# Linear attention and a gated FFN on one core: output weights loaded earlier, one undivided output projection for block 0, and an attention output tile laid out in column halves

## The chip, the core and the metric

The kernel runs on one NeuronCore of a Trainium2 chip. The metric is device time in microseconds, from launch to the end of the core's program. A profiled execution gives a trace of one run: its span is the time from the first to the last instruction that the profiler recorded. In the trace, PE is TensorE (PEld its weight loads), DVE is VectorE, ACT is ScalarE, POOL is GpSimd and SP is SyncE, which here only issues DMA transfers.

## The reference

There are two parts. The first is linear attention with decay, for batch 4, 8 heads, 768 positions and head size 64. With lam a decay of each head:

```python
for b in range(nb):
    intra = einsum('bhic,bhjc->bhij', qb, kb) * Dmask       # Dmask[i, j] = lam ** (i - j) for i >= j, else 0
    intra = einsum('bhij,bhjd->bhid', intra, vb)
    inter = einsum('bhid,bhde->bhie', qb * lam ** (pos + 1), kv_state)
    out[:, :, block b] = intra + inter
    kv_state = lam ** block * kv_state + einsum('bhsd,bhse->bhde', kb * lam ** (block - 1 - pos), vb)
```

The second part takes the attention output as x, with 3072 tokens (4 x 768) of 512 features (8 heads x 64):

```python
gate = 1 / (1 + exp(-(x @ w_gate)))      # w_gate: 512 x 1536
val = x @ w_val                          # w_val:  512 x 1536
out = (gate * val) @ w_out               # w_out:  1536 x 512
```

All inputs and the output are float32; the kernel computes with bfloat16 operands and accumulates in float32.

## The kernel before

**Tiling.** The sequence is cut into six blocks of 128 positions (n = 0 to 5), and a block is done for all four batches b together, so that a block has 512 tokens: batch b fills columns 128b to 128b + 127. The reference's block of 64 is an arrangement of its own; 128 gives the same function. Heads go in pairs, and the two heads of a pair use rows 0 to 63 and 64 to 127 of TensorE.

**Attention of a block** has these pieces. `t_` transposes k or q of two batches on TensorE (tk, tq in PSUM), `e_k` and `e_q` copy them out, to KS by ScalarE and to QS, with the decay factors, by VectorE. From block 2 on a DMA transpose (`xbar`, kt and qt) takes the place of `t_`. `piece_s` makes the scores (sp), `piece_m` multiplies them with the decay mask (MT, VectorE). `piece_i` multiplies q with the state Sb, `piece_a` adds scores times v (both into op), `piece_x` copies op to XT, the FFN's input, and `piece_c` makes the state's increment (cp) from v and from k scaled by `piece_kd` (kd, ScalarE). The list `att(n)` runs `piece_i`, `piece_a`, `piece_x` and `piece_c` in this order.

**FFN of a block.** There are 12 tiles of 128 hidden features. `piece_gv` (L343) makes one of them: four matmuls of 128x128 weights with 512 tokens into gp, four more into vp, a sigmoid by ScalarE (sg), and the product sg times vp by VectorE (ht). `piece_po` (L376) is the output projection: for each of four token tiles tt it accumulates 12 matmuls of 512 columns, one for each ht, into po, copies the sum to ob, and stores it from SP's DMA queue.

**Memory.** PSUM has two pools: ps_at with five buffers for attention and ps_ff with three for gp, vp and po. A new tile of a pool takes the buffer of the tile that came five or three tiles earlier, and waits until this has been read. Weights stay in SBUF: WG (gate), WV (value), WO (output).

**What sets the order.** The kernel fixes it by hand. Each engine runs its instructions in the order in which the program issues them; there is no planner. From L485 on, the order is a list `plan` of units: a unit is one `piece_gv` or one `piece_po`, with a list of further pieces that are issued right behind it. So attention of block n + 1 is threaded between the FFN tiles of block n.

**Loads.** Nearly all go through GpSimd's DMA queue, which casts float32 to bfloat16. They are issued in the order of the program and land in that order. The order of interest is that of L453 to L468: gate and value weights of the last tiles, block 1's k and q of batches 0 and 1, output weights 0 to 5, block 1's other k, q and v, output weights 6 to 11, then block 2's k and q. In blocks 1 to 5, k and q of batches 2 and 3 are loaded with the heads of a pair exchanged, in two transfers (L98). `next_loads` (L476) transposes a block's k and q by DMA from SP, then lets GpSimd wait for these (`gate`) and load v and the next k and q.

**The head.** Block 0 has no state. L399 to L449 run its attention with filler matmuls (`zeros`) between pieces, and end with batch 3 in two halves (ops), whose copies go to ScalarE and VectorE. Then `swap_halves` makes lamqs, lamq with the two 64-row halves exchanged, which `e_q` of block 1 uses.

**Around block 1.** In the plan (L530 to L571) block 1's first transposes and scores stand behind tiles 10 and 11 of block 0. Block 0's projection is cut in two: the first six hidden tiles (`lo`) of each token tile are projected right after block 0's tiles, with block 1's remaining attention between them, and copied to ob. The last six (`hi`) are projected behind block 1's second tile, and VectorE adds them to ob (L385). Block 0's stores are issued later, behind block 1's tile 3. Block 1's first tile is made in two column halves (L348): gate and value of columns 0 to 255, then of 256 to 511, since VectorE's copies of batches 2 and 3 come later than ScalarE's of 0 and 1.

Of the kernel before, what the change touches and what calls it, by code (L numbers as in the profile page):

```python
# [16 lines left out]
def kernel(  # L17
# [11 lines left out]
    nc = tc.nc  # L29
# [72 lines left out]
    def load_g(f0, f1):  # L102
        nc.gpsimd.dma_start(out=WG[:, :, f0 * 128:f1 * 128], in_=wg_r[:, :, f0 * 128:f1 * 128])  # L103

    def load_v(f0, f1):
        nc.gpsimd.dma_start(out=WV[:, :, f0 * 128:f1 * 128], in_=wv_r[:, :, f0 * 128:f1 * 128])  # L106
# [5 lines left out]
    def load_wo(f0, f1):  # L112
        nc.gpsimd.dma_start(out=WO[:, f0:f1], in_=wo_r[:, f0:f1])  # L113
# [94 lines left out]
    def tables_late():  # L208
        nc.scalar.activation(pk, lnl, AF.Exp, scale=jn[:, 0:1])
        nc.scalar.activation(kds, lnl, AF.Exp, scale=jn[:, 1:2])  # L210
        nc.scalar.activation(dec2, lnp, AF.Exp, scale=float(C))

    def swap_halves():
        ps = ps_at.tile([128, HP, C], FP32, name="lqs", tag="ps")
        nc.tensor.matmul(ps, lhsT=swap, rhs=lamq, start=True, stop=True)
        nc.vector.tensor_copy(lamqs, ps)

    def make_mask(u):
        nc.vector.tensor_tensor(
# [91 lines left out]

    def piece_x(n, bs, eng=None):
        if n not in XT:
            XT[n] = xtp.tile([128, NMT, B, C], BF16, tag="XT", name="XT")
        for b in bs:
            e = eng or (nc.vector if n < FIRST_XBAR and b >= NB2 else nc.scalar)
            (e.tensor_copy if e is nc.vector else e.copy)(XT[n][:, :, b, :], OP[n, b])  # L317

    def piece_c(n, hps):
        p, t = (ps_at, "ps") if n else (ps_ff, "ff")  # L320
        cp = p.tile([128, len(hps), B, 64], FP32, name="cp", tag=t)
        for i, hp in enumerate(hps):
            for b in range(B):
                for w in range(2):
                    h = 2 * hp + w
                    nc.tensor.matmul(cp[rows_of(half(b, h)), i, b, :],  # L326
                                     lhsT=KD[n][:, b, slot(n, b, h), :], rhs=T_["v", n][:, b, h, :],
                                     start=(i == 0 and b == 0), stop=(i == len(hps) - 1 and b == B - 1),
                                     skip_group_check=True)
        if n == 0:  # L330
            nc.scalar.copy(Sb[:, hps[0]:hps[-1] + 1], cp)
            return
        for i, hp in enumerate(hps):
            for at, d in ((slice(0, NB2), dec), (slice(NB2, B), decs)):
                nc.vector.scalar_tensor_tensor(  # L335
                    out=Sb[:, hp, at, :], in0=Sb[:, hp, at, :], scalar=d[:, hp:hp + 1],
                    in1=cp[:, i, at, :], op0=ALU.mult, op1=ALU.add)
# [4 lines left out]

    def piece_gv(n, ft):  # L343
        fs = slice(ft * 128, (ft + 1) * 128)
        x = XT[n].rearrange("p m b c -> p m (b c)")
        gp = ps_ff.tile([128, TCH], FP32, name="gp", tag="ff")
        parts = [slice(0, TCH)]
        if (n, ft) == (1, 0):  # L348
            parts = [slice(0, TCH // 2), slice(TCH // 2, TCH)]

        def product(ps, W, part):
            for mt in range(NMT):
                nc.tensor.matmul(ps[:, part], lhsT=W[:, mt, fs], rhs=x[:, mt, part],  # L353
                                 start=(part is parts[0] and mt == 0),
                                 stop=(part is parts[-1] and mt == NMT - 1), skip_group_check=True)

        product(gp, WG, parts[0])
        if len(parts) == 2:
            vp = ps_ff.tile([128, TCH], FP32, name="vp", tag="ff")
            product(vp, WV, parts[0])  # L360
            product(gp, WG, parts[1])
        sg = htp.tile([128, TCH], BF16, tag="sg", name="sg", bufs=3)
        nc.scalar.activation(sg, gp, AF.Sigmoid)  # L363
        if len(parts) == 1:
            vp = ps_ff.tile([128, TCH], FP32, name="vp", tag="ff")
        product(vp, WV, parts[-1])
        HT[n, ft] = htp.tile([128, TCH], BF16, tag="ht", name="ht", bufs=2 * NFT)
        nc.vector.tensor_mul(HT[n, ft], sg, vp)  # L368

    OB = {}  # L370

    def store(n, tt, c0=0, c1=DM):
        nc.sync.dma_start(out=out[tt * S + n * C:tt * S + (n + 1) * C, c0:c1],
                          in_=OB[n, tt][:, c0:c1])

    def piece_po(n, tt, c0, c1, eng, fts):  # L376
        if (n, tt) not in OB:
            OB[n, tt] = osb.tile([128, DM], FP32, tag="ob", name="ob")
        po = ps_ff.tile([128, DM], FP32, name="po", tag="ff")
        for ft in fts:  # L380
            nc.tensor.matmul(po[:, :c1 - c0], lhsT=HT[n, ft][:, tt * 128:(tt + 1) * 128],  # L381
                             rhs=WO[:, ft, c0:c1], start=(ft == fts[0]), stop=(ft == fts[-1]))
        o = OB[n, tt][:, c0:c1]
        if fts[0]:
            nc.vector.tensor_tensor(out=o, in0=o, in1=po[:, :c1 - c0], op=ALU.add)  # L385
        else:
            (eng.copy if eng is nc.scalar else eng.tensor_copy)(o, po[:, :c1 - c0])  # L387
        if n:
            store(n, tt, c0, c1)

# [2 lines left out]
    def zeros(m):  # L395
        for _ in range(m):
            nc.tensor.matmul(zps, lhsT=Sb[:, 0, 0:2, :], rhs=Sb[:, 0:2], start=True, stop=True)  # L397
# [38 lines left out]
    for b in range(3):  # L436
        piece_a(0, [b])
        piece_x(0, [b], nc.vector if b == 2 else nc.scalar)
    zeros(1)
    ops = [ps_at.tile([128, HP // 2, C], FP32, name="op", tag="ps") for _ in range(2)]  # L440
    for g in range(2):
        for hp in range(2 * g, 2 * g + 2):
            for w in range(2):
                nc.tensor.matmul(ops[g][rows_of(w), hp % 2, :], lhsT=T_["v", 0][:, 3, 2 * hp + w, :],
                                 rhs=MT[0, 3][:, w, hp, :], start=(hp % 2 == 0), stop=(hp % 2 == 1),
                                 skip_group_check=True)
    nc.scalar.copy(XT[0][:, 0:2, 3, :], ops[0])
    nc.vector.tensor_copy(XT[0][:, 2:4, 3, :], ops[1])
    swap_halves()  # L449

    for n in range(2):  # L453
        make_kd(n)
    load_gv(6, 8)
    load_g(8, 12)
    load_v(8, 10)
    load_v(10, 12)
    load(1, "k", 0, 2)
    load(1, "q", 0, 2)  # L460
    load_wo(0, 3)
    load_wo(3, 6)
    load(1, "k", 2, 4)
    load(1, "q", 2, 4)
    load(1, "v", 0, 2)
    load(1, "v", 2, 4)
    load_wo(6, 12)
    load(2, "kq")  # L468

    gates = const.tile([128, 2], BF16, tag="gates")  # L470
# [28 lines left out]
    def m_(n, b):  # L499
        return lambda: piece_m(n, b)  # L500

    def trans(n, bp):
        def go():
            bs = [2 * bp, 2 * bp + 1]
            t_("k", n, bs)
            e_k(n, bs)
            t_("q", n, bs)
            e_q(n, bs)
        return go
# [22 lines left out]
        behind[ft] = [kd(0, 2 * ft)]  # L532
    behind[1].append(lambda: make_mask(0))
    behind[3].append(lambda: make_mask(1))
    behind[10] = [trans(1, 0), kd(1, 0, 2, parts=[0])]
    behind[11] = [pair(piece_s, 1, 0), m_(1, 0), m_(1, 1), kd(1, 2, 6, parts=[0])]
    for ft in range(NFT):
        gv(0, ft, *behind[ft])
    lo, hi = range(NFT // 2), range(NFT // 2, NFT)
    po(0, 0, kd(1, 6, 8, parts=[0]), kd(1, 0, 2, parts=[1]), fts=lo)  # L540
    po(0, 1, t_k(1, [2, 3]), kd(1, 2, 5, parts=[1]), fts=lo, eng=nc.vector)
    po(0, 2, t_q(1, [2, 3]), pair(piece_c, 0, 0), pair(piece_c, 0, 1), kd(1, 5, 8, parts=[1]),
       pair(piece_s, 1, 1), m_(1, 2), m_(1, 3), fts=lo)
    po(0, 3, att(1), fts=lo)

    for n in range(1, NSTEP):
        nx = n + 1
        more = [[] for i in range(NFT)]
        if nx < NSTEP:
            more[3] = [lambda nx=nx: e_q(nx, [0, 1])]  # L550
            more[4] = [pair(piece_s, nx, 0), m_(nx, 0)]
            more[5] = [m_(nx, 1), lambda nx=nx: e_q(nx, [2, 3])]
            more[7] = [pair(piece_s, nx, 1), m_(nx, 2)]
            more[8] = [m_(nx, 3)]
            more[11] = [att(nx)]
        if nx < NSTEP - 1:
            for i in range(4):
                more[6 + i].append(kd(nx, 2 * i))
            more[5].append(lambda nx=nx: make_kd(nx))
        if n == 1:  # L560
            more[4:11] = more[3:10]
            more[3] = []
            more[2].append(lambda: next_loads(2))
            more[3].extend([lambda tt=tt, j=j: store(0, tt, 256 * j, 256 * j + 256)
                            for tt in range(B) for j in range(2)])
            more[8].append(lambda: next_loads(3))
        for ft in range(NFT):
            gv(n, ft, *more[ft])
            if (n, ft) == (1, 1):
                for tt in range(B):  # L570
                    po(0, tt, fts=hi)  # L571
        for tt in range(B):
            if n == NSTEP - 1 and tt == B - 1:
                po(n, tt, c=(0, 384), eng=nc.vector)
                po(n, tt, c=(384, 512))
            else:
                more = [lambda n=n: next_loads(n + 3)] if tt == B - 1 and n + 3 < NSTEP else []
                po(n, tt, *more)
# [35 lines left out]
```

## Time and profile before

| | |
|---|---|
| median of 11 runs | 228.34 us (227.86 to 228.6) |
| the profiled execution | 227.74 us |
| its span | 225.9 us |
| TensorE busy | 219.2 us |
| VectorE, ScalarE, GpSimd busy | 105.2, 101.1, 62.5 us |
| granted TensorE clock | 0.999 |
| first FFN matmul starts | 15.24 us |
| first output projection matmul starts | 37.56 us |
| block 1's first and third tile start | 47.65 and 56.30 us |
| last matmul's start | 221.8 us |

The times inside the span count from its start. A matmul's busy time is drawn to its modelled end, so that consecutive matmuls overlap in the record; the distance between two starts tells what one really costs. A row of a timeline gives start, duration, engine, line, operation, output and inputs, shapes, and how many instructions it merges; in brackets stands the idle time before it and what ended it. For a DMA, the row on POOL or SPq is only its issue; its landing is told by the time to landing of the view of its tile.

### The profile page before, as it was taken

The page shows a single profiled execution, that of the slowest core. Times are in us where ns is not written, and L with a number is a line of the kernel's source. Part 1 is how long each engine was busy: PE and PEld are TensorE (multiplying, and loading weights), DVE is VectorE, ACT ScalarE, POOL GpSimd, SP SyncE. Part 2 cuts the span into 40 slices and gives each one's busy share as a digit, 9 for nine tenths or more (in the row PEclk, how much of TensorE's full clock was granted, in tenths as well). Part 3 has the DMA queues.
Part 4 walks back from the last instruction along what each step waited for, and adds up shares of the span by engine and source line. Part 5 has one row for each costly group of instructions (what it writes and reads, how often), then busy time and mean ns, then how long its engine had stood idle before and what let it go on. Part 6 is the DMA issues. An engine that isn't in the chain of part 4 may idle for free.

```text
span 225.9 us, 4168 instructions
## 1 busy us (share of the span) xinstructions
PE 219.2 (97%) x1672; PEld 106.8 (47%) x1672; DVE 105.2 (47%) x192; ACT 101.1 (45%) x215; POOL 62.5 (28%) x81
## 2 busy tenths in 40 slices
PE   7899999999999999999999999999999999999993
PEld 2544445674444644444644444644444544444442
DVE  4775536595488601488410488420388400344200
ACT  5878336940348623348523348522333342333220
POOL 7999756800192048007600030000000000000000
PEclk9999999999999999999999999999999999999999
DMA  7999999999999969994993968012100012100022
GB/s 114 151 170 184 200 174 187 166 181 139 252 174 156 167 158 138 197 208 40 158 155 126 196 41 56 0 49 93 46 0 3 0 49 93 46 0 0 3 93 94
DMA packets 105459, 25.18 MB, mean 111 GB/s; under 512 B 97120, under 2 KB 103008, under 8 KB 105440
## 3 DMA queue, kind: packets, MB, share of 16 engines
q0 software_dynamic: 82400, 13.90, 79.6%
q1 hardware_dynamic: 22896, 11.01, 19.7%
q8 instruction: 13, 0.21, 0.4%
q14 instruction: 6, 0.05, 0.1%
q10 hardware_dynamic: 144, 0.00, 0.0%
HBM read 28.32 MB, written 6.29 MB: 153 GB/s over the span
## 4 chain that ended last, share of the span: by engine, by line
PE 81%; POOL 10%; DMA 6%; issue 1%; DVE 0%; ACT 0%; POOLq 0%
PE po L381 28%; PE gp L353 23%; PE vp L353 23%; DMA WO<-in_moe_w_out_dram 6%; POOL WV L106 3%; POOL WG L103 2%; PE op L307 2%; PE sp L276 2%; POOL qb L92 1%; POOL vb L92 1%; PE op L296 1%; POOL kb L92 1%; PE cp L326 1%; DVE QS L243 0%; POOL WO L113 0%
## 5 line engine op out<-in xcount | busy, mean ns | idle before, releaser
L368 DVE TENSOR_TENSOR ht<-sg,vp 128x512 bf16<-128x512 bf16 x72 | 49.4, 686 | 94.5 <-PE vp L353 94.5
L363 ACT ACTIVATE sg<-gp 128x512 bf16<-128x512 f32 x72 | 43.0, 597 | 70.5 <-PE gp L353 69.3
L353 PE MATMUL gp<-XT,WG 128*128 128x512 bf16 (+1 forms) x292 | 74.2, 377 | 0.0
L353 PE MATMUL vp<-XT,WV 128*128 128x512 bf16 (+1 forms) x292 | 74.1, 376 | 0.0
L381 PE MATMUL po<-WO,ht 128*128 128x512 bf16 (+2 forms) x300 | 63.9, 371 | 0.1
L353 PEld LDWEIGHTS <-WV 128*128 128x128 bf16 x292 | 28.3, 98 | 33.9 <-DMA WV<-in_moe_w_val_dram 0.7
L381 PEld LDWEIGHTS <-ht 128*128 128x128 bf16 x300 | 28.4, 98 | 32.6 <-issue 0.4
L353 PEld LDWEIGHTS <-WG 128*128 128x128 bf16 x292 | 27.8, 98 | 32.2 <-DMA WG<-in_moe_w_gate_dram 0.3
L387 ACT COPY ob<-po 128x512 f32<-128x512 f32 (+1 forms) x23 | 13.1, 571 | 41.1 <-PE po L381 39.1
L284 DVE TENSOR_TENSOR MT<-sp,mask 128x512 bf16<-128x512 f32 x48 | 30.4, 682 | 1.4 <-PE sp L276 1.4
L125 ACT ACTIVATE kd<-kb,kds 128x128 bf16<-128x128 bf16 (+1 forms) x72 | 24.0, 403 | 0.0
L474 POOL COPY gates<-kt 128x1 bf16<-128x1 bf16 x4 | 0.7, 186 | 51.5 <-DMA kt<-kb 51.5
L92 POOL DMA_DIRECT2D vb<-in_v_dram x9 | 11.9, 1332 | 3.1 <-issue 1.3
L317 ACT CAST XT<-op 128x512 bf16<-128x512 f32 x20 | 10.4, 597 | 5.1 <-PE op L307 5.1
L335 DVE SCALAR_TENSOR_TENSOR Sb<-Sb,dec,cp 128x128 bf16<-128x128 bf16 x32 | 8.6, 341 | 3.3 <-PE cp L326 3.3
L98 POOL DMA_DIRECT2D kb<-in_k_dram x10 | 8.9, 897 | 2.3 <-DMA WG<-in_moe_w_gate_dram 1.6
L92 POOL DMA_DIRECT2D qb<-in_q_dram x8 | 9.0, 1131 | 0.8 <-POOLq L598 0.8
L98 POOL DMA_DIRECT2D qb<-in_q_dram x10 | 8.9, 916 | 0.9 <-DMA WV<-in_moe_w_val_dram 0.9
L397 PE MATMUL zps<-Sb 128*128 128x512 bf16 x19 | 7.5, 528 | 1.5 <-DVE Sb L152 1.5
L92 POOL DMA_DIRECT2D kb<-in_k_dram x6 | 6.9, 1158 | 1.1 <-DMA WO<-in_moe_w_out_dram 1.1
L106 POOL DMA_DIRECT2D WV<-in_moe_w_val_dram x9 | 7.2, 816 | 0.0
L307 PE MATMUL op<-MT,vb 128*64 128x128 bf16 x184 | 6.3, 221 | 0.0
(60 smaller groups left out, 89.0 us busy)
## 6 DMA issues: line engine op xcount, KB each, us to landing
out_dram<-ob SPq DMA_DIRECT2D x19, 256.0 KB, 2.0
vb<-in_v_dram POOLq DMA_DIRECT2D x4, 512.0 KB, 7.3
qb<-in_q_dram POOLq DMA_DIRECT2D x6, 256.0 KB, 9.1
kb<-in_k_dram POOLq DMA_DIRECT2D x6, 256.0 KB, 8.4
qb<-in_q_dram POOLq DMA_DIRECT2D x12, 128.0 KB, 9.2
kb<-in_k_dram POOLq DMA_DIRECT2D x10, 128.0 KB, 9.1
out_dram<-ob SPq DMA_DIRECT2D x8, 128.0 KB, 1.9
vb<-in_v_dram POOLq DMA_DIRECT2D x3, 256.0 KB, 9.9
```

Of the source, the lines that this page charges most:

```text
L92: nc.gpsimd.dma_start(out=T_[c, n][:, b0:nat], in_=src[b0:nat, :, sl, :].rearrange("b h s d -> s (b h) d"))
L98: nc.gpsimd.dma_start(out=T_[c, n][:, m:b1, u::2, :], in_=src[m:b1, 1 - u::2, sl, :].rearrange("b h s d -> s (b h) d"))
L106: nc.gpsimd.dma_start(out=WV[:, :, f0 * 128:f1 * 128], in_=wv_r[:, :, f0 * 128:f1 * 128])
L125: nc.scalar.mul(KD[n][:, at, i, :], T_["k", n][:, at, i, :], kds[:, h:h + 1])
L284: nc.vector.tensor_tensor(out=MT[n, b][:, u], in0=SP[n, b][u], in1=(mask if n else mask0)[:, 1 - u if swapped(n, b) else u], op=ALU.mult)
L307: nc.tensor.matmul(OP[n, b][rows_of(w), hp, :], lhsT=T_["v", n][:, b, h, :], rhs=MT[n, b][:, slot(n, b, h) % 2, hp, :], start=(n == 0 and ...
L317: (e.tensor_copy if e is nc.vector else e.copy)(XT[n][:, :, b, :], OP[n, b])
L353: nc.tensor.matmul(ps[:, part], lhsT=W[:, mt, fs], rhs=x[:, mt, part], start=(part is parts[0] and mt == 0), stop=(part is parts[-1] and m ...
L363: nc.scalar.activation(sg, gp, AF.Sigmoid)
L368: nc.vector.tensor_mul(HT[n, ft], sg, vp)
L381: nc.tensor.matmul(po[:, :c1 - c0], lhsT=HT[n, ft][:, tt * 128:(tt + 1) * 128], rhs=WO[:, ft, c0:c1], start=(ft == fts[0]), stop=(ft == ft ...
L387: (eng.copy if eng is nc.scalar else eng.tensor_copy)(o, po[:, :c1 - c0])
```

## The change

The diff does six things.

1. The loads behind block 0's: gate and value weights of tiles 8 to 11 come in four transfers of equal size in turn; all output weights, now in four equal transfers, come ahead of the later halves of block 1's k and q and of its v.
2. Block 0's projection is one accumulation over 12 hidden tiles in one PSUM tile for each tt (`PO`), issued in two calls of six; the add in VectorE is gone. All of it, and block 1's attention between its parts, stands between block 0's last tile and block 1's first.
3. XT becomes two column halves of 256 tokens, [128, 2, 4, 256] in place of [128, 4, 4, 128]. A matmul over all 512 tokens reads two runs of 256.
4. Block 0's first tile makes its gate in two column halves, then the value as a whole. Block 1's first tile has the order that it had.
5. `swap_halves` goes ahead of batch 3's attention in the place of one filler matmul; its copy comes behind the attention's copies. The increment of the state of block 0 uses ps_at, and comes right behind block 0's tiles. Block 2's query scaling, scores and masks stand one tile later in block 1.
6. The very last store (128 columns) is issued by ScalarE and not by SP.

```diff
@@ -210,10 +210,11 @@
         nc.scalar.activation(kds, lnl, AF.Exp, scale=jn[:, 1:2])
         nc.scalar.activation(dec2, lnp, AF.Exp, scale=float(C))
 
+    lqs = []
+
     def swap_halves():
-        ps = ps_at.tile([128, HP, C], FP32, name="lqs", tag="ps")
-        nc.tensor.matmul(ps, lhsT=swap, rhs=lamq, start=True, stop=True)
-        nc.vector.tensor_copy(lamqs, ps)
+        lqs.append(ps_at.tile([128, HP, C], FP32, name="lqs", tag="ps"))
+        nc.tensor.matmul(lqs[0], lhsT=swap, rhs=lamq, start=True, stop=True)
 
     def make_mask(u):
         nc.vector.tensor_tensor(
@@ -311,14 +312,14 @@
 
     def piece_x(n, bs, eng=None):
         if n not in XT:
-            XT[n] = xtp.tile([128, NMT, B, C], BF16, tag="XT", name="XT")
+            XT[n] = xtp.tile([128, 2, NMT, TCH // 2], BF16, tag="XT", name="XT")
         for b in bs:
             e = eng or (nc.vector if n < FIRST_XBAR and b >= NB2 else nc.scalar)
-            (e.tensor_copy if e is nc.vector else e.copy)(XT[n][:, :, b, :], OP[n, b])
+            (e.tensor_copy if e is nc.vector else e.copy)(
+                XT[n][:, b // 2, :, b % 2 * C:(b % 2 + 1) * C], OP[n, b])
 
     def piece_c(n, hps):
-        p, t = (ps_at, "ps") if n else (ps_ff, "ff")
-        cp = p.tile([128, len(hps), B, 64], FP32, name="cp", tag=t)
+        cp = ps_at.tile([128, len(hps), B, 64], FP32, name="cp", tag="ps")
         for i, hp in enumerate(hps):
             for b in range(B):
                 for w in range(2):
@@ -342,51 +343,48 @@
 
     def piece_gv(n, ft):
         fs = slice(ft * 128, (ft + 1) * 128)
-        x = XT[n].rearrange("p m b c -> p m (b c)")
-        gp = ps_ff.tile([128, TCH], FP32, name="gp", tag="ff")
-        parts = [slice(0, TCH)]
-        if (n, ft) == (1, 0):
-            parts = [slice(0, TCH // 2), slice(TCH // 2, TCH)]
+        gp, vp = (ps_ff.tile([128, 2, TCH // 2], FP32, name=c, tag="ff") for c in ("gp", "vp"))
+        sg = htp.tile([128, TCH], BF16, tag="sg", name="sg", bufs=3)
+        whole, first, second = slice(0, 2), slice(0, 1), slice(1, 2)
 
         def product(ps, W, part):
             for mt in range(NMT):
-                nc.tensor.matmul(ps[:, part], lhsT=W[:, mt, fs], rhs=x[:, mt, part],
-                                 start=(part is parts[0] and mt == 0),
-                                 stop=(part is parts[-1] and mt == NMT - 1), skip_group_check=True)
-
-        product(gp, WG, parts[0])
-        if len(parts) == 2:
-            vp = ps_ff.tile([128, TCH], FP32, name="vp", tag="ff")
-            product(vp, WV, parts[0])
-            product(gp, WG, parts[1])
-        sg = htp.tile([128, TCH], BF16, tag="sg", name="sg", bufs=3)
-        nc.scalar.activation(sg, gp, AF.Sigmoid)
-        if len(parts) == 1:
-            vp = ps_ff.tile([128, TCH], FP32, name="vp", tag="ff")
-        product(vp, WV, parts[-1])
+                nc.tensor.matmul(ps[:, part], lhsT=W[:, mt, fs], rhs=XT[n][:, part, mt],
+                                 start=(part is not second and mt == 0),
+                                 stop=(part is not first and mt == NMT - 1), skip_group_check=True)
+
+        order = [(gp, WG, whole), (vp, WV, whole)]
+        if ft == 0 and n == 0:
+            order = [(gp, WG, first), (gp, WG, second), (vp, WV, whole)]
+        elif ft == 0 and n == 1:
+            order = [(gp, WG, first), (vp, WV, first), (gp, WG, second), (vp, WV, second)]
+        for ps, W, part in order:
+            product(ps, W, part)
+            if ps is gp and part is not first:
+                nc.scalar.activation(sg, gp.rearrange("p a b -> p (a b)"), AF.Sigmoid)
         HT[n, ft] = htp.tile([128, TCH], BF16, tag="ht", name="ht", bufs=2 * NFT)
-        nc.vector.tensor_mul(HT[n, ft], sg, vp)
-
-    OB = {}
+        nc.vector.tensor_mul(HT[n, ft], sg, vp.rearrange("p a b -> p (a b)"))
+
+    OB, PO = {}, {}
 
     def store(n, tt, c0=0, c1=DM):
-        nc.sync.dma_start(out=out[tt * S + n * C:tt * S + (n + 1) * C, c0:c1],
+        (nc.scalar if (n, tt, c1) == (NSTEP - 1, B - 1, DM) else nc.sync).dma_start(out=out[tt * S + n * C:tt * S + (n + 1) * C, c0:c1],
                           in_=OB[n, tt][:, c0:c1])
 
     def piece_po(n, tt, c0, c1, eng, fts):
         if (n, tt) not in OB:
             OB[n, tt] = osb.tile([128, DM], FP32, tag="ob", name="ob")
-        po = ps_ff.tile([128, DM], FP32, name="po", tag="ff")
+        if fts[0] == 0:
+            PO[n, tt] = ps_ff.tile([128, DM], FP32, name="po", tag="ff")
+        po = PO[n, tt]
         for ft in fts:
             nc.tensor.matmul(po[:, :c1 - c0], lhsT=HT[n, ft][:, tt * 128:(tt + 1) * 128],
-                             rhs=WO[:, ft, c0:c1], start=(ft == fts[0]), stop=(ft == fts[-1]))
-        o = OB[n, tt][:, c0:c1]
-        if fts[0]:
-            nc.vector.tensor_tensor(out=o, in0=o, in1=po[:, :c1 - c0], op=ALU.add)
-        else:
+                             rhs=WO[:, ft, c0:c1], start=(ft == 0), stop=(ft == NFT - 1))
+        if fts[-1] == NFT - 1:
+            o = OB[n, tt][:, c0:c1]
             (eng.copy if eng is nc.scalar else eng.tensor_copy)(o, po[:, :c1 - c0])
-        if n:
-            store(n, tt, c0, c1)
+            if n:
+                store(n, tt, c0, c1)
 
 
 
@@ -436,7 +434,7 @@
     for b in range(3):
         piece_a(0, [b])
         piece_x(0, [b], nc.vector if b == 2 else nc.scalar)
-    zeros(1)
+    swap_halves()
     ops = [ps_at.tile([128, HP // 2, C], FP32, name="op", tag="ps") for _ in range(2)]
     for g in range(2):
         for hp in range(2 * g, 2 * g + 2):
@@ -444,27 +442,27 @@
                 nc.tensor.matmul(ops[g][rows_of(w), hp % 2, :], lhsT=T_["v", 0][:, 3, 2 * hp + w, :],
                                  rhs=MT[0, 3][:, w, hp, :], start=(hp % 2 == 0), stop=(hp % 2 == 1),
                                  skip_group_check=True)
-    nc.scalar.copy(XT[0][:, 0:2, 3, :], ops[0])
-    nc.vector.tensor_copy(XT[0][:, 2:4, 3, :], ops[1])
-    swap_halves()
+    nc.scalar.copy(XT[0][:, 1, 0:2, C:], ops[0])
+    nc.vector.tensor_copy(XT[0][:, 1, 2:4, C:], ops[1])
+    nc.vector.tensor_copy(lamqs, lqs[0])
 
 
 
     for n in range(2):
         make_kd(n)
     load_gv(6, 8)
-    load_g(8, 12)
-    load_v(8, 10)
-    load_v(10, 12)
+    load_gv(8, 10)
+    load_gv(10, 12)
+    load_wo(0, 3)
+    load_wo(3, 6)
     load(1, "k", 0, 2)
     load(1, "q", 0, 2)
-    load_wo(0, 3)
-    load_wo(3, 6)
+    load_wo(6, 9)
+    load_wo(9, 12)
     load(1, "k", 2, 4)
     load(1, "q", 2, 4)
     load(1, "v", 0, 2)
     load(1, "v", 2, 4)
-    load_wo(6, 12)
     load(2, "kq")
 
     gates = const.tile([128, 2], BF16, tag="gates")
@@ -532,16 +530,18 @@
         behind[ft] = [kd(0, 2 * ft)]
     behind[1].append(lambda: make_mask(0))
     behind[3].append(lambda: make_mask(1))
-    behind[10] = [trans(1, 0), kd(1, 0, 2, parts=[0])]
-    behind[11] = [pair(piece_s, 1, 0), m_(1, 0), m_(1, 1), kd(1, 2, 6, parts=[0])]
+    behind[11] = [pair(piece_c, 0, 0), pair(piece_c, 0, 1)]
     for ft in range(NFT):
         gv(0, ft, *behind[ft])
     lo, hi = range(NFT // 2), range(NFT // 2, NFT)
-    po(0, 0, kd(1, 6, 8, parts=[0]), kd(1, 0, 2, parts=[1]), fts=lo)
-    po(0, 1, t_k(1, [2, 3]), kd(1, 2, 5, parts=[1]), fts=lo, eng=nc.vector)
-    po(0, 2, t_q(1, [2, 3]), pair(piece_c, 0, 0), pair(piece_c, 0, 1), kd(1, 5, 8, parts=[1]),
-       pair(piece_s, 1, 1), m_(1, 2), m_(1, 3), fts=lo)
-    po(0, 3, att(1), fts=lo)
+    po(0, 0, fts=lo)
+    po(0, 1, trans(1, 0), fts=lo)
+    po(0, 2, pair(piece_s, 1, 0), m_(1, 0), m_(1, 1), kd(1, 0, 4, parts=[0]), fts=lo)
+    po(0, 0, kd(1, 4, 8, parts=[0]), fts=hi)
+    po(0, 1, fts=hi)
+    po(0, 2, trans(1, 1), fts=hi)
+    po(0, 3, kd(1, 0, 8, parts=[1]), pair(piece_s, 1, 1), m_(1, 2), m_(1, 3), fts=lo)
+    po(0, 3, att(1), fts=hi)
 
     for n in range(1, NSTEP):
         nx = n + 1
@@ -554,21 +554,21 @@
             more[8] = [m_(nx, 3)]
             more[11] = [att(nx)]
         if nx < NSTEP - 1:
-            for i in range(4):
+            for i in range(4 if n > 1 else 0):
                 more[6 + i].append(kd(nx, 2 * i))
             more[5].append(lambda nx=nx: make_kd(nx))
         if n == 1:
-            more[4:11] = more[3:10]
-            more[3] = []
+            more[5:] = [more[3], more[4], more[5], [], more[7], more[8], []]
+            more[3], more[4] = [], []
+            for i in range(4):
+                more[7 + i].append(kd(nx, 2 * i))
+            more[11] = [att(nx)]
             more[2].append(lambda: next_loads(2))
             more[3].extend([lambda tt=tt, j=j: store(0, tt, 256 * j, 256 * j + 256)
                             for tt in range(B) for j in range(2)])
             more[8].append(lambda: next_loads(3))
         for ft in range(NFT):
             gv(n, ft, *more[ft])
-            if (n, ft) == (1, 1):
-                for tt in range(B):
-                    po(0, tt, fts=hi)
         for tt in range(B):
             if n == NSTEP - 1 and tt == B - 1:
                 po(n, tt, c=(0, 384), eng=nc.vector)
```

## The prediction

> **What bounds the kernel now.** I read the busy shares first, then the windows table cut at the stage borders, then the timelines of the one stage that differs.
>
> The page's first part:
>
> ```profile
> PE 219.2 (97%) x1672; PEld 106.8 (47%) x1672; DVE 105.2 (47%) x192; ACT 101.1 (45%) x215; POOL 62.5 (28%) x81
> ```
>
> TensorE is the bound. The stage table shows where it isn't full (columns: length of the stretch, busy time and instructions of each engine, granted clock, DMA engines' busy share, GB/s):
>
> ```profile
> 0.00:15.20 15.20, 12.65 (x116) 6.04 (x117) 10.52 (x27) 11.43 (x26) 14.04 (x26) 1.00 1.72 141
> 15.20:36.90 21.70, 21.67 (x113) 10.07 (x112) 10.21 (x16) 11.70 (x23) 16.35 (x20) 1.00 1.65 188
> 36.90:47.60 10.70, 10.45 (x201) 6.68 (x201) 7.58 (x13) 8.90 (x23) 6.50 (x7) 1.00 2.01 175
> 47.60:56.30 8.70, 8.70 (x52) 4.74 (x49) 6.07 (x15) 1.20 (x2) 0.00 (x0) 1.00 2.20 149
> 56.30:87.60 31.30, 31.30 (x258) 15.21 (x257) 15.53 (x29) 14.34 (x33) 13.69 (x16) 1.00 1.44 173
> ...
> 222.00:226.00 4.00, 0.00 (x0) 0.00 (x0) 0.00 (x0) 0.27 (x1) 0.00 (x0) 0.94 0.20 68
> ```
>
> From 56.3 us on TensorE has no gap that work of the change could fill; the clock is full. What can be won lies in the head (to 15.2), the first projection (36.9 to 56.3) and the 4 us behind the last matmul. "Busy" hides stalls, since a matmul is drawn with a pipelined end of 379 ns; so I go by starts. The TensorE timeline of that stage:
>
> ```profile
> 29.05 1.03 PE L353 MATMUL gp<-XT,WG 128*128 128x512 bf16 x4
> 29.96 1.04 PE L353 MATMUL vp<-XT,WV 128*128 128x512 bf16 x4
> ...
> 37.00 0.62 PE L276 MATMUL sp<-QS,KS 64*128 64x128 bf16 x16
> 37.56 3.02 PE L381 MATMUL po<-WO,ht 128*128 128x512 bf16 x12
> 40.41 0.61 PE L233 MATMUL tk<-ident,kb 128*128 128x128 bf16 x8
> ...
> 42.69 0.70 PE L326 MATMUL cp<-vb,kd 128*64 128x64 bf16 x32
> 43.54 0.62 PE L276 MATMUL sp<-QS,KS 64*128 64x128 bf16 x16 [0.16 <-DVE QS L243]
> ```
>
> Elsewhere four 512-column matmuls step by 0.863 us (0.2158 each). Four stalls stand out. 29.05 to 29.96 is 0.91: 0.05 too long, waiting for value weights. The 12 projection matmuls from 37.56 to 40.41 take 2.85 where 12 x 0.2158 is 2.59: 0.26 lost before the fourth, and the chain of waits ends its long transfer of output weights just there (landing at 38.43). The scores at 43.54 come 0.22 after the normal switch (32 state matmuls start from 42.69 to 43.19, a switch is about 0.13) and wait for VectorE's q scaling, which has only just got its transposes. The fourth is at 47.65: block 1's first gate matmul, 2.15 after the inter-block matmuls began at 45.50; the same sequence later in the run takes 2.09, so 0.06 for the copies of the attention output. Sum 0.59 us.
>
> **The change, part by part.** The sums are made against the profiled execution, 227.74 us (span 225.9 and 1.84 around it). The median is 228.34, 0.60 above it, so the profiled one is at the quick end; I carry the difference over to the median.
>
> *Head.* One filler matmul goes, the half-swap matmul takes its place during the wait for v, and its copy moves behind the attention copies. The first tile starts on columns 0 to 255. By TensorE's work that is 0.22 us earlier. But the first gate weights are issued at 9.9 and need 5.2 us: 15.15, and the first gate matmul is at 15.24 now. The weight load of the second tile's value product starts at 17.80 against a landing at 12.1 + 5.6 = 17.7, its matmul at 17.83, exactly on the 0.2158 pace. A quicker start would be given back there. VectorE's and GpSimd's queues up to these loads are unchanged. Taken 0; bounds -0.05 to +0.02 (the 8 half matmuls; see below).
>
> *Order of the loads.* GpSimd's queue, issues only:
>
> ```profile
> 22.18 1.16 POOL L92 DMA_DIRECT2D kb<-in_k_dram  x1
> 23.32 1.16 POOL L92 DMA_DIRECT2D qb<-in_q_dram  x1
> 24.45 1.53 POOL L113 DMA_DIRECT2D WO<-in_moe_w_out_dram  x2
> ...
> 36.80 0.83 POOL L113 DMA_DIRECT2D WO<-in_moe_w_out_dram  x1 [0.74 <-DMA WO<-in_moe_w_out_dram]
> ```
>
> The DMA engines are nearly full to 45 us and the landings are in order of issue, so I go by steps between landings (issue plus time to landing from the tile views): value weights (10 to 12) 31.2, k 32.9, q 34.6, output weights 36.55 and 38.4, k's other half 40.3, q's 41.9, v 43.5 and 45.2, output weights 6 to 12 49.1. So k and q halves cost 1.6 to 1.9, v 1.65, half the output weights 1.95 per 384 KB, and 3.9 for the 768 KB one. In the new order: 31.2, output weights 33.15 and 35.1, k 36.8, q 38.5, output weights 40.4 and 42.35, k's other half 44.25, q's 45.85, v 47.5 and 49.15; what comes after stays at its place. The gate load (8 to 12) is cut in two and the value load slips in between, so the value weights land a gate half earlier and the 0.05 stall at 29.96 goes.
>
> Against the cutting speaks the Trainium skill, "DMA: Bandwidth & Descriptors", sections "Anatomy of one DMA" and "Measured": each transfer has some 2.0 us of fixed cost, so batch to 1 MiB and more. Two more issues would by that be an estimated 4 us more, and output weights 9 to 12 would land at about 44 to 46. The rows decide otherwise: one load of 768 KB took 3.9 us of the queue, two of 384 KB 1.95 each; behind a full queue the fixed cost doesn't appear. I take the rows.
>
> *Projection 0.* 48 matmuls before and after; the second half moves from behind block 1's second tile to here, accumulating in its PSUM bank. Four VectorE adds (688 ns) and one VectorE copy go, one ScalarE copy (585 ns) comes; neither engine is on TensorE's path here. TensorE from 15.24 to block 1's third tile, by starts: 12 tiles x 8 x 0.2158 = 20.72; state matmuls standing alone 0.74 (0.09 switch, 0.50, 0.15 switch); 48 x 0.2158 = 10.36; two transposed pairs, 0.89 each (34.29 to 35.18), 1.79; scores 0.65 twice, 1.30; attention 0.09 + 2.15 (the 0.06 wait stays: XT's copies come behind the same matmuls), 2.24; block 1's tile in halves 1.74, and one tile 1.73. Sum 40.62. Before: 15.24 to 56.30, 41.06. Gain 0.44 us: 0.53 of stalls, less 0.09 for state matmuls that no longer share their switch.
>
> That holds if nothing new is late. Needed against landed, by the same count: output weights 0 to 6 from 36.7 on (35.1), first k and q 39.3 and 39.7 (36.8, 38.5), output weights 6 to 9 at 42.1 (40.4), 9 to 12 at 42.8 (42.35), second k 46.0 (44.25), second q 46.5 (45.85), v 50.8 (49.15 for the last, needed 51.3). The tight ones are 0.45 and 0.6. ScalarE, in its order: k copy 46.8 to 47.8 for scores at 48.2; eight k scalings (0.32 each when queued) to 50.3, then the last projection copy to 50.95 and XT from 51.3. VectorE's q copy is done at 47.8. All before TensorE needs them, by 0.35 at least. Bounds of this part: -0.6 to the late cases below.
>
> *XT's layout.* 568 whole gate and value matmuls now read two runs of 256 columns in place of one of 512. No row shows a moving operand in two runs. Lower bound 0. Upper bound: a break costs no more than a new instruction. Block 1's first tile shows that: 16 half matmuls took 1.742 where 8 whole ones take 1.726, 2.0 ns a break; 568 x 2.0 = 1.14 us. (The Trainium skill, "TensorE: Matmul & The Clock Gate", "Wait — 56ns, not 53.3ns?", puts 2.5 ns of fixed cost on each matmul, an estimated 1.4 us.) Both prices hang on the instruction, and their count doesn't change here; I take 0.
>
> *The scores of block 2* go one tile later on both VectorE and TensorE: 16 matmuls on the same path, and 1.7 us further from their transposes (q lands at 61.0). Nothing.
>
> *The last store* moves from SP's queue to ScalarE's.
>
> ```profile
> 221.36 0.56 DVE L387 COPY ob<-po 128x384 f32<-128x384 f32 x1 [8.96 <-PE po L381]
> 222.03 0.27 ACT L387 COPY ob<-po 128x128 f32<-128x128 f32 x1 [2.03 <-PE po L381]
> ...
> 220.02 3.10 SPq L373 DMA_DIRECT2D out_dram<-ob  x3
> ```
>
> The copy is done at 222.30, but SP, with the 384-column store before it, issues the last at 222.79; it lands 2.2 later, at 224.97, and the span ends 0.9 after that. ScalarE has nothing else to do: issue about 222.45, 0.35 us gained. The same skill page ("Issuing engines are not separate DMA queues") says that this only saves sequencer time, usually small; here all 0.49 of it is on the path. Bounds: ScalarE's only store-like row, the load of lam, took 3.1 to land; with that instead of 2.2 it is 0.55 lost; at best 0.49 and 0.3 of landing (1.9) won. I take 2.2, since its neighbours in size and place are the 1.9 to 2.2 of the other stores.
>
> **Sum**: 0 - 0.44 + 0 - 0.35 = -0.79: 226.95 for the profiled execution, 227.55 for the median.
>
> **Rivals.**
> *Late weights eat the block's gain* (likely end: the stall moves). For: margins of 0.45 and 0.6 on a queue that is full. Against: seven step sizes agree. Output weights 9 to 12 later by 0.9 cost 0.45: 228.0, no measurable change.
> *The queue slows more: slower than before.* The same 256 KB took 1.4 to 2.2 us between landings (k's second half, then block 2's first k). If the six loads between 31.2 and 42.35 all went at 2.2/1.7, they'd need 14.4 and weights 9 to 12 land at 45.6, 2.8 past need: 228.34 - 0.79 + 2.8 = 230.4. Break-even is a landing at 43.6; slower by the measurable bound from 44.05.
> *Two runs cost as a new matmul*: 227.55 + 1.14 = 228.7, within the bound. Against: one instruction.
> *More than counted*: the median lies 0.6 above the profiled execution; if that is more of the same stalls, they go too: 226.9.
>
> **How the numbers follow.** About 0.2% (0.46 us) is what a measurement of this kernel can tell. Likeliest case 58%, its own range 227.1 to 227.9; more than counted 8%; together faster 66%. Late weights 14% and two runs 8%: same 22%. Queue slows 12%: slower. The range 226.7 to 228.5 leaves out the slow queue, part of the two-runs case and a rest below.
>
> **What would show it.** Right: the first projection matmul near 36.7, 24 projection matmuls before the second transposes, no gap over 0.1 us inside the projection, block 1's third tile at about 55.9, whole matmuls still 0.2158 apart, and the last store issued by ScalarE some 0.15 after its copy. Wrong: a gap ahead of the 4th or 10th tile's projection matmul, a step of 0.217 or more for whole matmuls, or a last store that lands 3 us after its issue.

## The result

The changed kernel takes 227.02 us (median of 12 runs, 226.55 to 227.30). The kernel before takes 228.22 us over 47 runs beside it. The ratio is 0.9947, with a 95% interval of 0.9938 to 0.9955: 1.2 us faster (1.0 to 1.4). The forecast was 227.55, 0.79 us faster.

The profiled execution has a span of 224.8 us against 225.9, and TensorE is as full as before:

```profile
PE 218.9 (97%) x1675; PEld 106.9 (48%) x1675; DVE 101.9 (45%) x187; ACT 101.8 (45%) x216; POOL 63.9 (28%) x83
```

The changed kernel's windows, cut at its own stage borders (first gate matmul, state matmuls of block 0, block 1's first and third tile):

```profile
15.10:36.20 21.10, 20.94 (x100) 9.61 (x100) 9.61 (x15) 10.41 (x21) 15.68 (x21) 1.00 1.61 189
36.20:52.60 16.40, 16.40 (x241) 9.72 (x241) 7.70 (x13) 10.98 (x26) 8.71 (x9) 1.00 2.16 169
52.60:56.10 3.50, 3.50 (x27) 2.37 (x26) 3.29 (x11) 1.19 (x2) 0.00 (x0) 1.00 2.09 142
```

From 36.2 to 56.1 TensorE is busy throughout. Its timeline shows how:

```profile
15.16 1.05 PE L352 MATMUL gp<-XT,WG 128*128 128x256 bf16 x8 [0.28 <-DMA WG<-in_moe_w_gate_dram]
16.04 1.03 PE L352 MATMUL vp<-XT,WV 128*128 128x512 bf16 x4
16.90 1.03 PE L352 MATMUL gp<-XT,WG 128*128 128x512 bf16 x4
18.04 1.04 PE L352 MATMUL vp<-XT,WV 128*128 128x512 bf16 x4
...
36.27 0.70 PE L327 MATMUL cp<-vb,kd 128*64 128x64 bf16 x32
36.90 2.76 PE L381 MATMUL po<-WO,ht 128*128 128x512 bf16 x12
39.50 0.61 PE L234 MATMUL tk<-ident,kb 128*128 128x128 bf16 x8
...
42.33 4.06 PE L381 MATMUL po<-WO,ht 128*128 128x512 bf16 x18
46.23 0.61 PE L234 MATMUL tk<-ident,kb 128*128 128x128 bf16 x8
...
56.09 1.03 PE L352 MATMUL gp<-XT,WG 128*128 128x512 bf16 x4
```

Twelve projection matmuls from 36.90 to 39.50 take 2.60 us, where they took 2.85; the 18 from 42.33 take 3.90, 0.2167 each. Four whole gate or value matmuls still take 0.86 (16.04 to 16.90). But the second tile's value product starts 1.14 us after its gate product (16.90 to 18.04) where 0.86 is the pace: 0.28 us of wait for its weights, which land at 18.0, that the kernel before did not have in its profile.

The last rows, around the two last stores:

```profile
221.15 0.56 DVE L385 COPY ob<-po 128x384 f32<-128x384 f32 x1 [8.96 <-PE po L381]
221.74 0.33 SPq L371 DMA_DIRECT2D out_dram<-ob  x1
221.82 0.27 ACT L385 COPY ob<-po 128x128 f32<-128x128 f32 x1 [2.03 <-PE po L381]
222.12 0.35 ACTq L371 DMA_DIRECT2D out_dram<-ob  x1
```

ScalarE issues the last store at 222.12, 0.03 us after its copy's end. It lands 1.8 us later, where it was issued 0.49 after the copy and took 2.2. Behind the start of the last matmul stand 3.23 us; before, 4.11.

So the profiled spans, 225.88 and 224.80, differ like this: head to the second value product +0.21 (17.83 to 18.04), from there to block 1's third tile -0.42 (38.47 to 38.05), from there to the last matmul 0.00, tail -0.87; sum -1.08.

### The profile page after: what moved, and what is told of

Read it like the earlier page. It is cut to its first block, busy times and chain, and to the rows that moved or that the text cites. A ratio compares the mean times of both kernels' runs of the same rounds, so it can differ in the third digit from the quotient of the medians.

```text
span 224.8 us, 4166 instructions
## 1 busy us (share of the span) xinstructions
PE 218.9 (97%) x1675; PEld 106.9 (48%) x1675; DVE 101.9 (45%) x187; ACT 101.8 (45%) x216; POOL 63.9 (28%) x83
## 4 chain that ended last, share of the span: by engine, by line
PE 91%; POOL 4%; DMA 3%; issue 1%; ACT 0%; POOLq 0%
PE po L381 28%; PE vp L352 27%; PE gp L352 27%; DMA WV<-in_moe_w_val_dram 3%; PE sp L277 2%; PE op L308 2%; POOL vb L92 1%; PE op L297 1%; PE cp L327 1%; POOL qb L92 1%; POOL WG L103 1%; POOL kb L92 1%; PE tk L234 0%; PE tq L234 0%; POOL WV L106 0%
## 5 line engine op out<-in xcount | busy, mean ns | idle before, releaser
L385 ACT COPY ob<-po 128x512 f32<-128x512 f32 (+1 forms) x24 | 13.7, 572 | 41.9 <-PE po L381 39.9
L103 POOL DMA_DIRECT2D WG<-in_moe_w_gate_dram x8 | 6.4, 805 | 0.5 <-issue 0.5
```

## The experiments

The theory after the result: the first projection gives the 0.4 that was forecast, the tail twice its forecast, and the head neither gains nor loses by the edit. The rival: the tail gives its 0.35, and the plan gives 0.85. In the next two expectations, A is the first of these and B the second.

**The tail alone, on the kernel before.**

```diff
-        nc.sync.dma_start(out=out[...],
+        (nc.scalar if (n, tt, c1) == (NSTEP - 1, B - 1, DM) else nc.sync).dma_start(out=out[...],
```

> The kernel before with one edit: the last 128-column store is issued from ScalarE. The profile of the changed kernel has 3.2 us behind the last matmul's start where there were 4.05. Theory A (the tail is worth what the profile shows): 0.85 us faster than before, about 227.4. Theory B (the prediction's size: issue 0.35 earlier, landing unchanged): 0.35 us faster, about 227.9. In the profile the store should be issued within 0.05 us of its copy's end and land in 1.8 (A) or 2.2 us (B).

227.58 us against 228.18; ratio 0.9974 (0.9965 to 0.9982): 0.59 us faster (0.41 to 0.80). In its profile 3.28 us stand behind the last matmul's start, the issue comes 0.03 after the copy, and the store lands 1.8 later:

```profile
222.18 0.33 SPq L373 DMA_DIRECT2D out_dram<-ob  x1
222.27 0.27 ACT L387 COPY ob<-po 128x128 f32<-128x128 f32 x1 [2.03 <-PE po L381]
222.56 0.35 ACTq L373 DMA_DIRECT2D out_dram<-ob  x1
```

The profile is A's; the timed gain lies half-way between the two, and its interval excludes both 0.35 and 0.85. A's size came from one pair of profiles, and that of the kernel before has the longest tail of all. With SP's last store the four profiles have 4.11, 4.10, 4.03 and 3.93 us; with ScalarE's, seven have 3.23 to 3.28, and an eighth, with the old loads, 3.39. The means without that eighth differ by 0.79, just inside the timed interval.

**The change without its tail.**

```diff
-        (nc.scalar if (n, tt, c1) == (NSTEP - 1, B - 1, DM) else nc.sync).dma_start(out=out[...],
+        nc.sync.dma_start(out=out[...],
```

> The changed kernel with the last store back on SP. A: what is left of 1.2 us is the first projection's 0.4, so 0.35 us faster than before, about 227.85, and the tail in the profile is 4.05 us again. B: 0.85 us faster than before, about 227.35.

227.59 us; ratio 0.998 (0.9969 to 0.9991): 0.46 us faster (0.2 to 0.7). The store's rows are those of before:

```profile
221.68 1.19 SPq L371 DMA_DIRECT2D out_dram<-ob  x2
```

SP needs 1.19 us for two stores, the second issue at 222.53 for a copy that ends at 222.03; it lands 2.1 us later. The tail is 4.03 us again. That is A: the rest of the change is worth what the forecast said, 0.44, within its interval. The two parts, 0.59 and 0.46, add up to 1.05 of the whole's 1.2, within their intervals.

**XT in column halves alone, on the kernel before.**

```diff
-            XT[n] = xtp.tile([128, NMT, B, C], BF16, tag="XT", name="XT")
+            XT[n] = xtp.tile([128, 2, NMT, TCH // 2], BF16, tag="XT", name="XT")
...
-                nc.tensor.matmul(ps[:, part], lhsT=W[:, mt, fs], rhs=x[:, mt, part],
+                nc.tensor.matmul(ps[:, part], lhsT=W[:, mt, fs], rhs=XT[n][:, part, mt],
```

> The kernel before with XT in column halves alone; every whole matmul reads two runs of 256 columns. Theory A (the fixed cost hangs on the instruction): unchanged within 0.2 us, whole matmuls 0.2158 us apart. Rival (a break costs as a new instruction): 1.1 us slower, 0.2178 us apart.

228.23 us; ratio 1.0002 (0.9994 to 1.0011). Two runs of 256 columns cost nothing: the rival's 1.1 us would be a ratio of 1.005. This profile also shows a wait that the profile of the kernel before did not have, ahead of block 1's second k transposes:

```profile
41.22 0.61 PE L233 MATMUL tk<-ident,kb 128*128 128x128 bf16 x8 [0.31 <-DMA kb<-in_k_dram]
```

k's second half lands at 41.1 us here and at 40.2 there. This is not the layout's doing, for the profile with the tail alone has it too, with k at 40.5: its transposes start 3.08 us after the first projection matmul, where the kernel before took 2.85.

```profile
37.57 3.01 PE L381 MATMUL po<-WO,ht 128*128 128x512 bf16 x12
40.65 0.61 PE L233 MATMUL tk<-ident,kb 128*128 128x128 bf16 x8
```

The old plan thus had a further tight point, which cost up to half a microsecond. In the changed kernel k lands at 44.3 and is needed at 46.2. From the second value product to block 1's third tile the three profiles with the old plan and loads took 38.47 (the kernel before), 38.73 (tail alone) and 38.99 us (XT alone); all seven with the new plan and loads took 38.04 or 38.05. The profile of the kernel before was the quickest of the three there.

**The old head in the changed kernel.**

```diff
-    swap_halves()
+    zeros(1)
     ops = [...]
...
+    swap_halves()
     nc.vector.tensor_copy(lamqs, lqs[0])
...
-        if ft == 0 and n == 0:
-            order = [(gp, WG, first), (gp, WG, second), (vp, WV, whole)]
-        elif ft == 0 and n == 1:
+        if ft == 0 and n == 1:
```

> The changed kernel with the old head: filler matmul in its old place, half-swap matmul after batch 3, first tile's gate over all columns. Theory A (the second value tile's weights set the pace, whenever the first tile starts): same as the changed kernel within 0.1 us, 1.2 us faster than before, second value product at its landing. Rival (the earlier first matmul is worth what TensorE saves): 0.15 to 0.25 us slower than the changed kernel, 1.0 us faster than before.

226.83 us; ratio 0.994 (0.9928 to 0.9952): 1.4 us faster than before (1.1 to 1.6), not told apart from the changed kernel, and the rival's 1.0 lies just outside. Its second value product waits for the same weights, and longer:

```profile
15.02 1.02 PE L352 MATMUL gp<-XT,WG 128*128 128x512 bf16 x4
...
18.32 1.04 PE L352 MATMUL vp<-XT,WV 128*128 128x512 bf16 x4 [0.55 <-DMA WV<-in_moe_w_val_dram]
```

The edits of the head are worth nothing that these runs can tell, as forecast. The wait of 0.28 us in the changed kernel's profile is no result of these edits either: it is longer without them.

**Fewer, larger loads in the changed kernel.**

```diff
-    load_gv(8, 10)
-    load_gv(10, 12)
+    load_g(8, 12)
+    load_v(8, 10)
+    load_v(10, 12)
...
-    load_wo(6, 9)
-    load_wo(9, 12)
+    load_wo(6, 12)
```

> The changed kernel with the loads in fewer pieces: output weights 6 to 11 as one transfer at the same place, gate weights of tiles 8 to 11 as one ahead of their value weights. If behind a full queue a transfer has no fixed cost: the one large transfer lands when the second of the two did (42.6 us), so projection 6 to 8 at 42.3 waits 0.3 us, and the value weights of tile 8 wait 0.05 as in the kernel before: 0.3 us slower than the changed kernel, 0.9 us faster than before. If each transfer had 2 us of fixed cost: two fewer land everything 2 to 4 us earlier, no wait, same as the changed kernel.

227.0 us; ratio 0.9959 (0.9946 to 0.9973), 0.93 us faster than before (0.6 to 1.2). The interval overlaps that of the changed kernel, so the time decides nothing. The landings do. The one transfer of 768 KB lands 3.83 us after the q load ahead of it (38.62 to 42.45); the two of 384 KB land 1.72 and 1.77 after theirs (39.11, 40.83, 42.60), 3.49 in all. In the six other profiles with the two transfers they took 3.77 to 4.19 from the q load's landing, and in all five with one transfer it took 3.76 to 3.83 after the load ahead of it. There is no fixed cost of 2 us for each transfer in this full queue; a second transfer cost some 0.4 us at most. The wait of 0.3 us forecast at the projection did not come: in this profile all of TensorE's work ran 0.15 us later (state matmuls at 36.42), and the projection's sixth tile was reached at 42.49, just behind the landing.

**Plan and loads apart.** The changed kernel with the old order of loads, and the kernel before with the new one (both edits are the load lines of the diff alone):

> The changed kernel with the old order of the loads; the plan alone. Output weights 6 to 11 then land at 49.1 us and are needed at 42.3: 6.8 us of wait in the projection, of which nothing comes back later: about 233.5 to 234, 5.5 us slower than before. If the projection's place were what brings the gain, and not the loads, the wait would be under 1 us.

> The kernel before with the new order of the loads; the loads alone. The 0.05 and 0.26 us waits at tile 8 and in the first projection go, but block 1's second k is needed at 40.1 us and lands at 44.3 (with 12.6 to 13.1 us to landing as in the changed kernel): 4 us of wait, with second q and v behind it: 3.5 to 5 us slower than before, about 232.

235.38 and 233.96 us against 228.07 (one run each): 7.3 and 5.9 us slower, both more than expected. The old loads under the new plan:

```profile
38.58 2.10 PE L381 MATMUL po<-WO,ht 128*128 128x512 bf16 x9 [0.89 <-DMA WO<-in_moe_w_out_dram]
...
49.07 0.58 PE L381 MATMUL po<-WO,ht 128*128 128x512 bf16 x1 [5.64 <-DMA WO<-in_moe_w_out_dram]
49.87 4.48 PE L381 MATMUL po<-WO,ht 128*128 128x512 bf16 x14 [0.22 <-issue]
```

There are two waits, the second as expected at the landing of weights 6 to 11 (49.0). And the matmuls after it step by 0.427 us, twice the usual. The granted clock, the third column from the end in the windows, tells why:

```profile
44.00:49.00 5.00, 0.00 (x0) 0.00 (x0) 1.72 (x3) 0.00 (x0) 0.71 (x1) 0.67 1.56 193
49.00:53.00 4.00, 3.71 (x10) 1.46 (x11) 0.00 (x0) 1.18 (x4) 0.00 (x0) 0.57 2.44 156
```

The clock went to half about 2.2 us into the wait and stayed there for some 3 us after it. The new loads under the old plan failed at another place than expected:

```profile
36.94 0.64 PE L233 MATMUL tk<-ident,kb 128*128 128x128 bf16 x8 [2.55 <-DMA kb<-in_k_dram]
38.61 1.04 PE L233 MATMUL tq<-ident,qb 128*128 128x128 bf16 x8 [1.04 <-DMA qb<-in_q_dram]
```

Not k's second half but its first is late: the old plan transposes it behind tile 10, at 34.2 us, and it lands at 36.9. Here too the clock fell to half, from 37.4 to 44.2:

```profile
39.00:42.00 3.00, 2.78 (x13) 1.35 (x11) 0.69 (x1) 0.82 (x3) 2.14 (x2) 0.50 1.50 193
```

Neither part stands alone: the loads must come in the order in which the plan needs them.

**GpSimd's queue in the head.**

```diff
     load(0, "k", 2, 4)
...
-    nc.gpsimd.affine_select(out=tri, in_=tri, ...)
     load(0, "q", 2, 3)
...
     for ft in range(4):
         load_gv(ft, ft + 1)
+    nc.gpsimd.affine_select(out=tri, in_=tri, ...)
     load_g(4, 6)
```

> The changed kernel with GpSimd's making of tri (0.29 us on its queue, needed first at 19.5 us) moved behind the weights of the first four tiles, so that v and these weights are issued 0.29 us earlier. Theory A (the head is set by GpSimd's issues and the landing behind them): first gate weights at 14.9 and the second value weights 0.25 us earlier, so 0.2 to 0.3 us faster than the changed kernel, 1.45 us faster than before. Rival (the DMA engines' rate sets these landings, or the attention of batch 3 does): under 0.1 us.

226.76 us; ratio 0.9942 (0.9929 to 0.9954): 1.3 us faster than before (1.0 to 1.6), which holds the times of both theories. The landings speak for the rival. The weights were issued 0.4 us earlier, the first gate weights at 9.51, but landed at 14.94, only 0.17 earlier, and the second tile's value weights, issued at 11.7, took 6.4 us and landed at 18.1, no earlier than in the changed kernel (18.0). An issue 0.4 us earlier did not bring their landing forward.

**What makes those weights late.** In ten of the eleven profiles of the kernels so far, old heads and new, this load lands 1.1 to 1.9 us after the one ahead of it, where most loads around it step by 0.7 to 0.8. By the trace's DMA records, a DMA of 16 KB on the instruction queue (here called a fetch) starts at 15.5 to 16.2 us in all of them and holds one engine for 0.9 us. There are 13 in a run, on average 250 instructions of TensorE apart (matmuls and weight loads), but single distances go from 44 to 481. In those ten, the weights land 2.0 to 2.3 us after its start, and by and large a later start goes with a later landing. To move it, the fillers were cut into more instructions:

```diff
-    zeros(9)
+    for _ in range(9):
+        for i in range(4):
+            nc.tensor.matmul(zps[:, i * 128:(i + 1) * 128], lhsT=Sb[:, 0, 0:2, :],
+                             rhs=Sb[:, 0, 0:2, :], start=True, stop=True)
```

> The changed kernel with each of the first nine filler matmuls cut into four of 128 columns: 54 more instructions on TensorE ahead of everything, the same columns. In the profiles so far a DMA of 16 KB on the instruction queue starts whenever TensorE has run some 256 instructions, first at 15.5 to 16.2 us, takes 0.9 us of one DMA engine, and the second tile's value weights land 2.1 to 2.3 us after its start. If this fetch is what makes them late: the fetch starts 54 instructions earlier, at 13 to 14 us, another load ahead of them lands late (by 0.5 to 1.2 us), these weights land 0.74 us after the load before them, at 17.3, and the second value product starts 0.22 us after its predecessor. Rival (something else makes just these weights late): they land at 17.8 to 18.3 as before. The time: within 0.4 us of the changed kernel either way, since another load of the head is hit instead.

> The changed kernel once more, beside the one with more TensorE instructions, as its control: 1.2 us faster than before; first instruction fetch at 15.5 to 16.2 us, second tile's value weights 2.1 to 2.3 us after its start, 24 projection matmuls without a gap.

227.21 us, ratio 0.9956 (0.994 to 0.9973), and 226.82 us for the control, 0.9941 (0.9924 to 0.9958). The first fetch moved to 14.77, less far than expected. The value product of the second tile did not wait in the one, and did in the other:

```profile
17.55 1.03 PE L352 MATMUL gp<-XT,WG 128*128 128x512 bf16 x4
18.41 1.03 PE L352 MATMUL vp<-XT,WV 128*128 128x512 bf16 x4
```

```profile
16.85 1.03 PE L352 MATMUL gp<-XT,WG 128*128 128x512 bf16 x4
18.18 1.04 PE L352 MATMUL vp<-XT,WV 128*128 128x512 bf16 x4 [0.30 <-DMA WV<-in_moe_w_val_dram]
```

But in the first, block 0's k load of batches 2 and 3, well ahead of the fetch, landed 0.7 us later than in the control (9.95 against 9.26), and all loads behind it were as late, up to these weights. From the first gate weights on the steps were an even 0.70 to 0.76; no single load behind the fetch was hit, though the theory had it so. The kernel with fewer loads did the same from its first v on, by 0.5 us, and its second value weights were not hit either, though the fetch came at 16.24. Two things can be said: these loads have about half a microsecond of lateness that comes at one place or another, and the fetch goes with it in ten profiles. That the fetch causes it is not shown, and what delays the early loads in the other two is open.

One more thing shows when the profiles are set side by side. The second value product starts later with the change: at 17.81 to 18.12 us in the three with the old plan and loads (mean 17.92), at 17.98 to 18.32 in the six with the new ones and the fillers uncut (mean 18.14). The two that mix them fit: 17.81 with the old plan, 18.01 with the new. The edits of the head do not explain this 0.22 us, for the old head in the changed kernel is the latest of the six. Whether another part of the change causes it, or chance in so few profiles, is open.

## Why the prediction was right, and where it was not

*The bound and the place of the gain* were right: block 1's third tile and the last matmul are 165.48 us apart in both profiles.

*The first projection*, forecast 0.44 us, is 0.42 between the profiles of the kernel before and the changed one, and the timed runs without the tail show 0.46 (0.2 to 0.7). That the numbers agree so well is in part luck. The forecast counted the stalls of one profile, the one with the fewest; against the mean of the three (38.73 us) the plan and its loads gain 0.68, and the later second value product, which the forecast took at nothing, gives 0.22 back. The steps behind the forecast held: the waits for output weights, for the value weights of tile 8 and for the scaled q are gone, the state matmuls alone take 0.63 from 36.27, and the wait of 0.06 at block 1's first gate stayed (2.15 us from 50.47 to 52.62). The first projection matmul and block 1's third tile came 0.2 later than forecast (36.90 and 56.09), by the wait in the head. The landings were forecast by adding steps between landings. For the loads from output weights to v the forecast was 33.15, 35.1, 36.8, 38.5, 40.4, 42.35, 44.25, 45.85, 47.5, 49.15; measured were 33.35, 35.2, 36.9, 39.1, 40.8, 42.6, 44.3, 46.0, 47.7, 49.3. None is off by more than about 0.6, and all were in time, the tightest, output weights 9 to 12, by about 0.4, and by 0.2 in the profile of the control. One reading for the slower queue was off: k's second half came in two transfers, of which 1.4 us was the first; its 256 KB took 1.8 (38.43 to 40.22), and block 2's first k 2.3 (49.05 to 51.34). That case did not arise.

*Cutting loads*: behind this full queue no cost of 2 us for each transfer appears in the landings, against the rule of the Trainium skill that was weighed ("DMA: Bandwidth & Descriptors", "Anatomy of one DMA").

*XT's two runs cost nothing*: shown, to within 0.25 us by the timed interval.

*The head*: worth nothing, as forecast, but for a shorter reason than given. It was said to be exactly on the pace of the second value weights; these land at 17.8 to 18.3 us in the profiles, and this decides. It cost 0.21 between those two profiles, for which the bounds of the term (-0.05 to +0.02) left no room.

*The tail* is the term that was mis-sized: "0.35 us gained" was 0.87 between those two profiles, 0.79 between the means of all, and 0.59 (0.41 to 0.80) in the timed runs. Two steps were off. The issue was set at 222.45, 0.15 after the copy: ScalarE fired 0.03 after its copy, so that 0.46 of the 0.49 came back. The larger miss is the landing. It was kept at 2.2 and took 1.8, less than the 1.9 of the best bound; SP's last store took 2.0 to 2.2 in four profiles, ScalarE's 1.8 in seven. The section of the Trainium skill that is quoted there ("Issuing engines are not separate DMA queues", in "DMA: Bandwidth & Descriptors") has only sequencer time saved; here the landing shortened as well, and why is not shown. The trace had nearer rows for both steps: 0.03 between copy and issue in SP's own store just before, 1.9 and 2.0 in the landings of its last but one and last but two.

The rival of *more than counted* came true in part: the further wait at the second k in two of three profiles of the old plan is such a loss, and the new plan has it in none of seven. How often it comes in other executions is not shown.

## What to carry to other kernels

When an engine's queue issues two stores close together at the very end, try giving the last one to the engine that made its data: here issue and landing both shortened. Behind a full DMA queue, add the steps between landings, not times from issue to landing, to forecast a new order of loads, and set them against when each is needed; a plan and its order of loads have to be changed together. And when a head waits on loads that land just in time, look at several profiles before crediting or blaming an edit for a few tenths; the same holds for the profile that a forecast counts its stalls in.

## What was not expected of the hardware

Two stores from one SP queue were issued 0.84 us apart although the second's data was ready 0.49 earlier; from ScalarE's queue the same 64 KB store was issued 0.03 us after its data and landed in 1.8 instead of 2.0 to 2.2 us. The granted clock was half, with 0.427 us for a 512-column matmul, from 2.2 us into a wait of TensorE of 5.64 us until 3 us after it; and from just after a wait of 2.55 us, over one of 1.04, until 5.6 us after that. A DMA of 16 KB on the instruction queue comes 13 times in a run and holds a DMA engine for 0.9 to 1.5 us.
